# Softmax weights divided by their row sums before the turn, in an attention plus two-MLP kernel

## The chip, the cores and the metric

One core of a Trainium2 chip runs the whole program. The metric is device time in microseconds, from launch to end. The profiled execution also has a span, from its first to its last instruction.

## The reference

```python
def _attn_ref(q, k, v, tau):            # q, k, v: 4 x 8 heads x 576 x 64, fp32
    scale = 1.0 / np.sqrt(q.shape[-1])
    scores = scale * np.matmul(q, k.transpose(0, 1, 3, 2))
    thresh = np.max(scores, axis=-1, keepdims=True) - tau
    scores = np.where(scores >= thresh, scores, -1000000000.0)
    scores = scores - np.max(scores, axis=-1, keepdims=True)
    attn = np.exp(scores)
    attn = attn / (np.sum(attn, axis=-1, keepdims=True) + 1e-09)
    return np.matmul(attn, v)
# reference: x = attention out as 2304 x 512
#   x = elu(x @ moe_w_in) @ moe_w_out        (512 -> 2048 -> 512)
#   out = leaky(x @ moe2_w_in) @ moe2_w_out  (512 -> 2048 -> 512)
```

## The kernel before

The work on attention is cut into 144 *units* (64 queries of two heads at once, so 128 partitions of scores against 576 keys) and 32 *groups* (4 or 5 units of one pair of heads; GROUPS, NE pairs in each). `group` (L417) loads k, q and v of the pair through SyncE's DMA queue (L423, L424, L426) and calls `unit` (L434) for each unit:

- TensorE multiplies q by k into PSUM tile s (L442);
- VectorE scales it into SBUF tile ss and finds the row extreme nm (L446); thr is nm plus tau on GpSimd or VectorE (L449, L451);
- ScalarE applies the threshold with a steep Prelu (L454) and the exponential into tile e, with the row's sum accumulated into a column of su (L457);
- the weights have to be turned so that keys lie on partitions. In the four pairs of the first group index (GP=1) TensorE does it (L472); in the other 28 groups VectorE turns e in blocks of 32 by 32 into t (L464), and 16 DMAs for each group, issued by SyncE, move the 32-partition blocks from t to their place in p (L486).

Then TensorE multiplies p by v into PSUM (L496). The row sums go another way: `row_sums` (L509) takes reciprocals of the group's sums (L511), turns them (L512), stores them in DRAM (L513), and after that has landed reads them back in two DMAs, spread over 64 partitions each (L515), into rb. VectorE multiplies the product by rb into x (L504). Each group so has 22 DMAs on SyncE's queue: 3 loads, 16 for p, 3 for the sums.

The first MLP's products on TensorE (h at L548, y at L591) use three fp32r passes with the hidden half of the weights that is loaded first. Seven blocks of 256 tokens (BESIDE) of them run beside the attention; what is left of the MLPs runs after it. Weights come raw from DRAM (L317) and are split into a high and a low part by GpSimd, ScalarE and VectorE (L321 to L341).

The order is not written by hand: `Order.run` (L110) is a list scheduler that runs when the kernel is built. It holds a cost and a due time (vt, shifted by the constants in KN) for each operation, lets some choose among engines by letters in KN (A ScalarE, D VectorE, P GpSimd), and fixes the order of instructions on every engine. For SyncE it takes ISSUE = 350 ns for each DMA. On the chip each engine, SyncE included, works through its list in order, and an instruction that has to wait holds all behind it. Tiles come from rings: k, q, v, p, t, e and s have two buffers each, ss has three, the product in PSUM one.

Of the kernel before, what the change touches and what calls it, by code (L numbers as in the profile page):

```python
# [10 lines left out]
F32 = mybir.dt.float32  # L11
F32R = mybir.dt.float32r
U32 = mybir.dt.uint32
AF = mybir.ActivationFunctionType
ALU = mybir.AluOpType
# [3 lines left out]
B, H, S, D = 4, 8, 576, 64  # L19
NT, DM, DFF = B * S, H * D, 2048  # L20
NH = B * H
NP = NH // 2
NE = H // 2
HALF = S // 2
# [5 lines left out]
NU = S // 64  # L30
GROUPS = [(b, u0, u1) for b in range(B) for u0, u1 in ((0, 4), (4, NU))]
UM = 5
WT = 32 * UM
BESIDE = 7
GP = 1
SX = 640
LAG = 2
# [5 lines left out]
KN = dict(  # L43
    pad=18, stay=3577.21, late=1.3, margin=0, look=0.00390102, warm=3, tu=2231.35, lead=16053.3, wv0=828.315,
    wv1=194.793, early=4257.91, boff=24778.1, bdt=4649.72, yoff=2581.02, coff=-6478.49, wb=1663.97, w2a=5835.19,
    o1=-2909.85, o2=1357, o3=2931.81, o4=-3826.63, o5=5331.7, o6=-25.7749, mo=-10678.1, ka='PA', kl='PAD', kh='PA',
    ko='D', kt='DP', kx='A', kxl='DP', km='DP', kg='AD', kgl='P', kgl1='D', kd='P', kc='AD')

PE, ACT, DVE, POOL, SP, HOST = "PE", "ACT", "DVE", "POOL", "SP", "HOST"
# [40 lines left out]
class Order:  # L90
# [5 lines left out]
    def op(self, alts, deps=(), uses=(), vt=0.0, lat=0.0):  # L96
        o = Op()
        o.alts = alts if isinstance(alts, list) else [alts]
        o.deps, o.vt, o.lat = [d for d in deps if d is not None], vt, lat
        o.outs, o.done, o.eng, o.seq = [], None, None, len(self.ops)  # L100
        for g in uses:
            if g.back is not None:
                o.deps.append(g.back)
            if not g.users and g.before is not None:
                o.deps.append(g.before.users[0])
            g.users.append(o)
        self.ops.append(o)
        return o

    def run(self):  # L110
        for o in self.ops:
            deps = set()
            for d in o.deps:
                deps.update(d.users if isinstance(d, Gen) else (d,))
            deps.discard(o)
            o.deps, o.left = list(deps), len(deps)
            for d in o.deps:
                d.outs.append(o)
# [17 lines left out]
        while left:  # L136
            best = None
            for e in engines:
                while soon[e] and (soon[e][0][4].done is not None or soon[e][0][0] <= free[e]):
                    t, vt, seq, k, o = heapq.heappop(soon[e])  # L140
# [14 lines left out]
            start, e = best  # L155
            while soon[e] and soon[e][0][0] <= start:
                t, vt, seq, k, o = heapq.heappop(soon[e])
# [8 lines left out]
            vt, seq, k, o = heapq.heappop(now[e])  # L166
# [50 lines left out]
def dve(n):  # L217
    return 69 + 1.042 * n


def dve2(n):
    return 69 + 0.521 * n
# [3 lines left out]
LAND = 2100.0  # L226
ISSUE = 350
HALFP = 105
# [6 lines left out]
def pool_ts(n):  # L235
    return 162 + 0.832 * n
# [12 lines left out]
def moved(packets, size):  # L249
    return packets * (6 + size * 0.0385) / 16 * 1.35  # L250

@with_exitstack
def attn_moe_kernel(ctx, tc, qT, kT, vn, tau, w1i, w1o, w2i, w2o, yp, rsd, out):
    nc = tc.nc
    od = Order()
    op = od.op
# [4 lines left out]
    def ring(pool, n, shape, dtype, tag):  # L261
        return Ring(lambda dt=dtype: (pool[0] if isinstance(pool, list) else pool).tile(shape, dt, tag=tag, name=tag, bufs=n), n)
# [6 lines left out]
    x = const.tile([128, KC, NT], F32, name="x")  # L269
# [18 lines left out]
    PORT = True  # L288

    def sp(packets, size, fn):  # L290
        return (SP, ISSUE, fn, moved(packets, size))

    def pick(who, **alts):
        names = {"A": ACT, "D": DVE, "P": POOL}
        return [(names[c], *alts[c]) for c in who]
# [12 lines left out]
    def copy_of(who, n, dst, src, half=0):  # L308
        return pick(who, A=(actp(n) + 50 * half, lambda: nc.scalar.copy(out=dst(), in_=src())),  # L309
                    D=(dve(n) + HALFP * half, lambda: nc.vector.tensor_copy(dst(), src())))  # L310
# [44 lines left out]
    ya = Ring(lambda: psm.tile([128, 2, 512], F32, tag="y", name="y", bufs=1), 1)  # L355
    s_r = Ring(lambda: psa.tile([128, 2, 512], F32, tag="s", name="s", bufs=2), 2)
    v_ps = Ring(lambda: psa.tile([128, 512], F32, tag="v", name="v", bufs=1), 1)

    ac = sbuf(aes, "ac")
    ap_ = sbuf(aes, "attn")  # L360
    rings = {True: moe_rings(sbuf(aes, "ma"), TA)}
    k_r = ring(ap_, 2, [128, 2, HALF], F32, "k")
    q_r = ring(ap_, 2, [128, 2, 64 * UM], F32, "q")
    v_r = ring(ap_, 2, [128, 2, 5, D], F32, "v")
# [3 lines left out]
    ss_r = Ring(None, 3)  # L368
    es_ = [ac.tile([128, SX], F32, name=f"e{j}") for j in range(2)]
    for t in es_:  # L370
        nc.gpsimd.memset(t[:, S:SX], 0.0)
    e_r = Ring(itertools.cycle(es_).__next__, 2)
    ident = ac.tile([128, 128], F32, name="ident")
    make_identity(nc, ident)
    sm_r = {t: ring(ap_, 4, [128, 1], F32, t) for t in ("nm", "thr")}
    su_r = ring(ap_, 3, [128, UM], F32, "su")
    rc_r = Ring(None, 2)
    st_r = ring(ap_, 2, [128, 32], F32, "st")
    rb_r = ring(ap_, 2, [128, 64 * UM], F32, "rb")

# [5 lines left out]
    ss_r.make = itertools.cycle(sts).__next__  # L386
    sus = [ac.tile([128, 32], F32, name=f"rc{j}") for j in range(2)]
    for t in sus:
        nc.vector.memset(t, 1.0)
    rc_r.make = itertools.cycle(sus).__next__  # L390
    wz = sts[0]
# [22 lines left out]
    xready = {}  # L414
    slot = itertools.count()

    def group(gi, p, vts):  # L417
        b, u0, u1 = GROUPS[gi]
        n, hp = u1 - u0, b * NE + p
        w = 32 * n  # L420
        due = vts[0] - KN["lead"]
        k, q, v = k_r.new(), q_r.new(), v_r.new()
        ld = [op(sp(128, 2304, lambda: nc.sync.dma_start(out=k(), in_=kT[hp])), [], [k], due),  # L423
              op(sp(256, 256 * n, lambda: nc.sync.dma_start(  # L424
                  out=q()[:, :, 0:64 * n], in_=qT[hp][:, :, 64 * u0:64 * u1])), [], [q], due)]
        lv = op(sp(128, 2560, lambda: nc.sync.dma_start(out=v(), in_=vn[hp])), [], [v], due + 8e3)  # L426
        by_pe = gi < GP
        su, pg, tg = su_r.new(), p_r.new(), None if by_pe else t_r.new()
        done, turned = [], []

# [3 lines left out]
        def unit(j, vt):  # L434
            s, ss, e = s_r.new(), ss_r.new(), e_r.new()
            nm, thr = (sm_r[t].new() for t in ("nm", "thr"))

            def qk():
                for h in range(2):
                    for i in range(2):  # L440
                        r = slice(64 * i, 64 * i + 64)
                        nc.tensor.matmul(s()[64 * h:64 * h + 64, i, 0:HALF], q()[r, h, 64 * j:64 * j + 64],  # L442
                                         k()[r, h], start=True, stop=True)
# [13 lines left out]
            o = op((ACT, act(S) + 190, lambda: nc.scalar.activation(  # L457
                out=e()[:, 0:S + 1], in_=ss()[:, 0:S + 1], func=AF.Exp, bias=taun, accum_out=su()[:, j:j + 1])),
                [o], [ss, e, su], vt + KN["o2"])
            done.append(o)  # L460
            cols = slice(32 * j, 32 * j + 32)

            if not by_pe:
# [3 lines left out]
                return  # L467
            t = ya.new()

# [12 lines left out]
        vt = vts[n - 1] + KN["o3"]  # L482
        rb, rgot = row_sums(gi * NE + p, n, su, done, vt + 500)
        got = turned
        if not by_pe:
            got = [op(sp(32, 20 * w, lambda a=a, d=d: nc.sync.dma_start(  # L486
                out=pg()[32 * d:32 * d + 32, 5 * a * w:5 * a * w + 5 * w],
                in_=tg()[32 * a:32 * a + 32, 5 * d * w:5 * d * w + 5 * w])), turned, [pg, tg], vt + KN["o4"])
                for a in range(4) for d in range(4)]
            vt += KN["o5"]  # L490
# [10 lines left out]
        def split(a):  # L501
            return a.rearrange("p (h u i) -> p h u i", h=2, i=32)

        xready[gi, p] = op((DVE, dve(64 * n), lambda: nc.vector.tensor_tensor(  # L504
            out=x[:, p, b * S + 64 * u0:b * S + 64 * u1].rearrange("p (u h i) -> p h u i", h=2, i=32),
            in0=split(ps()[:, 0:64 * n]), in1=split(rb()[:, 0:64 * n]), op=ALU.mult)),
            [o, *rgot], [ps, rb], vt + KN["o6"] + 500)

    def row_sums(at, n, su, done, vt):  # L509
        rb, st, rc = rb_r.new(), st_r.new(), rc_r.new()  # L510
        o = op((DVE, 140, lambda: nc.vector.reciprocal(out=rc()[:, 0:n], in_=su()[:, 0:n])), done, [su, rc], vt)  # L511
        o = op((DVE, 140, lambda: nc.vector.transpose(out=st(), in_=rc())), [o], [rc, st], vt)  # L512
        o = op(sp(128, 128, lambda: nc.sync.dma_start(out=rsd[at].rearrange("a u i -> (a u) i"), in_=st())),  # L513
               [o], [st], vt)
        got = [op(sp(128, 128 * n, lambda h=h: nc.sync.dma_start(  # L515
            out=rb()[64 * h:64 * h + 64, 0:64 * n].rearrange("p (a q) -> p a q", a=2),
            in_=rsd[at, 2 * h:2 * h + 2, 0:n].rearrange("a u i -> a (u i)").partition_broadcast(64))),
            [o], [rb], vt) for h in range(2)]
        return rb, got

# [256 lines left out]
```

## Time and profile before

| | us |
|---|---|
| median of 3 runs | 1160.18 |
| the three runs | 1159.62, 1160.18, 1168.07 |
| profiled execution, its own time | 1164.52 |
| its span | 1162.7 |
| TensorE busy, by the page | 1051.9 |

The profiled execution is 4.3 us above the median of the runs. Engines are called PE (TensorE), PEld (its weight loads), DVE (VectorE), ACT (ScalarE), POOL (GpSimd) and SP (SyncE). SPq rows are DMA issues on SyncE: their length is the time of the issue, not of the transfer. "x16" is a run of 16 merged instructions. An arrow names what the idle time ended on.

### The profile page before, as it was taken

The numbers are of one execution on the slowest core, as the hardware profiler recorded it, in microseconds if no ns is written. First come the engines' busy times: TensorE is split into PE (matmuls) and PEld (weight loads), VectorE is DVE, ScalarE is ACT, GpSimd is POOL, SyncE is SP. The second block draws the span as 40 slices with busy tenths as digits, with TensorE's granted clock in tenths as the row PEclk, the third lists the DMA queues.
The fourth block names the chain that finished last, engine by engine and source line by source line (L and its number), as shares of the span: only waits on it lengthen the run. The fifth ranks groups of instructions, "written<-read, shape, count | busy, mean of one in ns | idle before, by whom it ended". The sixth has DMA issues, their size and how long they took to land.

```text
span 1162.7 us, 17064 instructions
## 1 busy us (share of the span) xinstructions
PE 1051.9 (90%) x6294; PEld 814.4 (70%) x6294; DVE 586.6 (50%) x1201; ACT 508.0 (44%) x1006; POOL 157.5 (14%) x278
## 2 busy tenths in 40 slices
PE   7778777787788778889999999999999999999998
PEld 3455455555566555558888888988888888888898
DVE  6876555655566556628888943686121121121121
ACT  6976555555455555515655532453221221221221
POOL 3454121222111122100111100010000000000000
PEclk9989898989899889989999999999999999999999
DMA  6676666656666666543544411132000000000000
GB/s 217 195 214 178 171 179 178 176 136 179 158 176 158 162 178 176 152 123 109 161 132 161 146 36 37 56 120 79 1 37 1 1 37 1 1 37 1 1 37 20
DMA packets 72435, 125.39 MB, mean 108 GB/s; under 512 B 16032, under 2 KB 37024, under 8 KB 72352
## 3 DMA queue, kind: packets, MB, share of 16 engines
q1 hardware_dynamic: 72352, 124.30, 37.9%
q8 instruction: 50, 0.82, 0.3%
q14 instruction: 33, 0.27, 0.1%
HBM read 72.35 MB, written 9.96 MB: 71 GB/s over the span
## 4 chain that ended last, share of the span: by engine, by line
PE 65%; SPq 15%; DMA 9%; DVE 5%; issue 3%; ACT 2%; POOL 0%; DVEq 0%; ACTq 0%; POOLq 0%
PE y L591 29%; PE h L548 15%; PE hb L548 13%; SPq L486 13%; PE v L496 6%; DMA rb<-rsd_dram 2%; DMA rsd_dram<-st 2%; DMA wraw<-in_w1i_dram 2%; PE s L442 2%; DVE ss L446 2%; DMA p<-t 2%; DVE t L464 1%; ACT e L457 1%; SPq L515 1%; SPq L426 1%
## 5 line engine op out<-in xcount | busy, mean ns | idle before, releaser
L591 PE MATMUL y<-gh,woh 128*128 128x512 f32 (+1 forms) x736 | 255.6, 347 | 2.1 <-ACT ysx L309 1.4
L591 PE MATMUL y<-gl,woh 128*128 128x512 f32 (+1 forms) x736 | 251.4, 342 | 0.0
L591 PE MATMUL y<-gh,wol 128*128 128x512 f32 (+1 forms) x736 | 251.3, 341 | 0.0
L298 DVE TENSOR_TENSOR gl<-g,gh 128x512 fp32r<-128x512 f32 (+1 forms) x128 | 83.3, 651 | 270.6 <-ACT g L574 260.9
L496 PE MATMUL v<-p,v 128*64 128x320 f32 (+1 forms) x640 | 127.9, 496 | 68.8 <-DMA rsd_dram<-st 39.1
L548 PE MATMUL h<-xh,wih 128*128 128x256 f32 (+1 forms) x480 | 164.6, 343 | 14.1 <-DVE g L567 9.4
L591 PEld LDWEIGHTS y<-gh,woh 128*128 128x128 f32 x736 | 138.5, 188 | 34.7 <-issue 14.4
L548 PE MATMUL h<-xl,wih 128*128 128x256 f32 (+1 forms) x480 | 159.0, 331 | 1.3 <-POOL xl L299 1.0
L548 PE MATMUL h<-xh,wil 128*128 128x256 f32 (+1 forms) x480 | 158.3, 330 | 0.0
L454 ACT ACTIVATE ss<-ss,thr 128x576 f32<-128x576 f32 x144 | 110.3, 768 | 105.5 <-DVE thr L451 58.2
L591 PEld LDWEIGHTS y<-gl,woh 128*128 128x128 f32 x736 | 138.6, 188 | 16.2
L591 PEld LDWEIGHTS y<-gh,wol 128*128 128x128 f32 x736 | 138.6, 188 | 16.2
L496 PEld LDWEIGHTS v<-p,v 128*64 128x64 f32 x640 | 62.7, 162 | 122.5 <-issue 64.1
L446 DVE TENSOR_SCALAR_CACHE_REDUCE ss<-s,scl 128x576 f32<-128x576 f32 x144 | 115.1, 800 | 46.6 <-PE s L442 45.3
L464 DVE STREAM_TRANSPOSE t<-e 128x640 f32<-128x640 f32 x128 | 106.7, 839 | 44.7 <-DMA rsd_dram<-st 19.0
L548 PEld LDWEIGHTS h<-xh,wih 128*128 128x128 f32 x480 | 91.6, 191 | 43.4 <-DVE g L567 12.3
L457 ACT ACTIVATE e<-ss,taun 128x577 f32<-128x577 f32 x144 | 111.5, 774 | 13.4 <-DVE t L464 11.1
L442 PE MATMUL s<-k,q 64*64 64x288 f32 x1152 | 97.6, 442 | 12.9 <-DVE ss L446 8.7
L548 PEld LDWEIGHTS h<-xl,wih 128*128 128x128 f32 x480 | 91.8, 191 | 10.2 <-POOL xl L299 1.5
L548 PEld LDWEIGHTS h<-xh,wil 128*128 128x128 f32 x480 | 91.9, 191 | 8.2
L548 PE MATMUL hb<-xl,wih 128*128 128x512 f32 (+1 forms) x256 | 94.5, 369 | 0.0
L548 PE MATMUL hb<-xh,wil 128*128 128x512 f32 (+1 forms) x256 | 94.5, 369 | 0.0
(438 smaller groups left out, 1139.7 us busy)
## 6 DMA issues: line engine op xcount, KB each, us to landing
p<-t SPq DMA_DIRECT2D x256, 100.0 KB, 2.2
p<-t SPq DMA_DIRECT2D x192, 80.0 KB, 2.4
v<-in_vn_dram SPq DMA_DIRECT2D x32, 320.0 KB, 3.7
k<-in_kT_dram SPq DMA_DIRECT2D x32, 288.0 KB, 3.0
wraw<-in_w1i_dram SPq DMA_DIRECT2D x16, 512.0 KB, 4.4
wraw<-in_w1o_dram SPq DMA_DIRECT2D x16, 512.0 KB, 3.6
wraw<-in_w2i_dram SPq DMA_DIRECT2D x16, 512.0 KB, 3.5
wraw<-in_w2o_dram SPq DMA_DIRECT2D x16, 512.0 KB, 3.4
```

What stands on the lines that cost most here:

```text
L298: return pick(who, D=(dve(n), lambda: nc.vector.tensor_tensor(**args()), PORT), P=(pool_tt(n), lambda: nc.gpsimd.tensor_tensor(**args())))
L426: lv = op(sp(128, 2560, lambda: nc.sync.dma_start(out=v(), in_=vn[hp])), [], [v], due + 8e3)
L442: nc.tensor.matmul(s()[64 * h:64 * h + 64, i, 0:HALF], q()[r, h, 64 * j:64 * j + 64], k()[r, h], start=True, stop=True)
L446: o = op((DVE, dve(S) + 160, lambda: nc.vector.tensor_scalar(out=ss()[:, 0:S].rearrange("p (j c) -> p j c", j=2), in0=s()[:, :, 0:HALF], s ...
L454: o = op((ACT, act(S) + 95, lambda: nc.scalar.activation(out=ss()[:, 0:S], in_=ss()[:, 0:S], func=AF.Prelu, bias=thr(), scale=-1.0, alpha= ...
L457: o = op((ACT, act(S) + 190, lambda: nc.scalar.activation(out=e()[:, 0:S + 1], in_=ss()[:, 0:S + 1], func=AF.Exp, bias=taun, accum_out=su( ...
L464: turned.append(op((DVE, dve(SX) + 70, lambda: nc.vector.transpose(out=blocks(tg).rearrange("p d c q -> p c d q")[:, :, :, cols], in_=e(). ...
L486: got = [op(sp(32, 20 * w, lambda a=a, d=d: nc.sync.dma_start(out=pg()[32 * d:32 * d + 32, 5 * a * w:5 * a * w + 5 * w], in_=tg()[32 * a:3 ...
L496: nc.tensor.matmul(ps()[64 * h:64 * h + 64, 0:64 * n], v()[:, h, c, :], blocks(pg)[:, 2 * h:2 * h + 2, c], start=(c == 0), stop=(c == 4))
L515: got = [op(sp(128, 128 * n, lambda h=h: nc.sync.dma_start(out=rb()[64 * h:64 * h + 64, 0:64 * n].rearrange("p (a q) -> p a q", a=2), in_= ...
L548: nc.tensor.matmul(hp(), w_()[:, cs], x_()[:, 0:tb], start=(k == 0 and z == 0), stop=(k == KC - 1 and z == 2))
L591: nc.tensor.matmul(ysl(yg, m), w_()[:, cs], g_()[:, 0:tb], start=(first and z == 0 and share == 0), stop=(last and z == 2 and end))
```

## The change

In each unit a reciprocal of the row's sum is taken on VectorE (128 by 1), and GpSimd multiplies the 576 columns of e by it in place, before e is turned (the scheduler knows a VectorE form too; the constant kn is 'P', so GpSimd has all of them). `row_sums` and its DRAM tensor, its three DMAs a group, its reciprocal and small transpose are gone; the product is copied from PSUM to x by ScalarE (kv='A') where VectorE multiplied. e has three buffers. q is laid out in DRAM by groups, so that a load has 128 packets of 512n bytes where it had 256 of 256n. The 16 block moves are listed by target quarter first. The scheduler's cost of a DMA issue is 400 ns, and 640 ns for block moves, and the constants in KN are others: thr is taken by VectorE alone (kt), the high part of g by ScalarE alone (kg), the high part of x by ScalarE or VectorE (kx), the low bits of the weights by ScalarE or VectorE (kl), and due times differ. The code for moves issued by ScalarE (NA) and for more groups turned by TensorE (PT, AHEAD) is not in use: NA is 0 and PT is empty.

```diff
 KN = dict(
-    pad=18, stay=3577.21, ..., ka='PA', kl='PAD', kh='PA',
-    ko='D', kt='DP', kx='A', kxl='DP', km='DP', kg='AD', kgl='P', kgl1='D', kd='P', kc='AD')
+    pad=18, stay=455.902, ..., ka='PA', kl='AD',
+    kh='PAD', ko='D', kt='D', kx='AD', kxl='DP', km='DP', kg='A', kgl='P', kgl1='D', kd='P', kc='AD', kn='P', kv='A')
...
-ISSUE = 350
+ISSUE = 400
...
-    q_r = ring(ap_, 2, [128, 2, 64 * UM], F32, "q")
+    q_r = ring(ap_, 2, [128, 128 * UM], F32, "q")
...
-    es_ = [ac.tile([128, SX], F32, name=f"e{j}") for j in range(2)]
+    es_ = [ac.tile([128, SX], F32, name=f"e{j}") for j in range(3)]
...
-              op(sp(256, 256 * n, lambda: nc.sync.dma_start(
-                  out=q()[:, :, 0:64 * n], in_=qT[hp][:, :, 64 * u0:64 * u1])), [], [q], due)]
+              op(sp(128, 512 * n, lambda: nc.sync.dma_start(
+                  out=q()[:, 0:128 * n], in_=qT[hp][:, 128 * u0:128 * u1])), [], [q], due)]
...
-                out=e()[:, 0:S + 1], in_=ss()[:, 0:S + 1], func=AF.Exp, bias=taun, accum_out=su()[:, j:j + 1])),
+                out=e()[:, 0:S + 1], in_=ss()[:, 0:S + 1], func=AF.Exp, bias=taun, accum_out=su())),
                 [o], [ss, e, su], vt + KN["o2"])
-            done.append(o)
+            o = op((DVE, 150, lambda: nc.vector.reciprocal(out=su(), in_=su())), [o], [su], vt + KN["o2"])
+            o = op(pick(KN["kn"], P=(pool_ts(S) + 90, lambda: nc.gpsimd.tensor_scalar(
+                            out=e()[:, 0:S], in0=e()[:, 0:S], scalar1=su(), scalar2=1.0, op0=ALU.mult, op1=ALU.mult)),
+                        D=(dve2(S), lambda: nc.vector.tensor_scalar(
+                            out=e()[:, 0:S], in0=e()[:, 0:S], scalar1=su(), scalar2=None, op0=ALU.mult), PORT)),
+                   [o], [su, e], vt + KN["o3"])
...
-        rb, rgot = row_sums(gi * NE + p, n, su, done, vt + 500)
         got = turned
         if not by_pe:
-            got = [op(sp(32, 20 * w, ...)) for a in range(4) for d in range(4)]
+            for z, (a, d) in enumerate((a, d) for d in range(4) for a in range(4)):
...
+                    got.append(op(sp(32, 20 * w, lambda copy=copy: copy(nc.sync), 640), turned, [pg, tg],
+                                  vt + KN["o4"]))
...
-        xready[gi, p] = op((DVE, dve(64 * n), lambda: nc.vector.tensor_tensor(
-            out=x[...], in0=split(ps()[:, 0:64 * n]), in1=split(rb()[:, 0:64 * n]), op=ALU.mult)),
-            [o, *rgot], [ps, rb], vt + KN["o6"] + 500)
-
-    def row_sums(at, n, su, done, vt):
...
+        xready[gi, p] = op(copy_of(KN["kv"], 64 * n, lambda: x[...], lambda: split(ps()[:, 0:64 * n])),
+                           [o], [ps], vt + KN["o6"] + 500)
```

## Rows read from the trace of the kernel before

**Rows 1.** The page: the busy time of each engine, its share of the span, instructions.

```profile
PE 1051.9 (90%) x6294; PEld 814.4 (70%) x6294; DVE 586.6 (50%) x1201; ACT 508.0 (44%) x1006; POOL 157.5 (14%) x278
```

**Rows 2.** Windows: us, busy PE, PEld, DVE, ACT, POOL, PEclk, DMA share, GB/s.

```profile
0.00:65.00 65.00, 47.89 (x386) 24.31 (x386) 49.87 (x134) 51.17 (x106) 28.40 (x44) 0.94 0.66 204
65.00:515.00 450.00, 362.53 (x2824) 250.21 (x2820) 256.05 (x601) 238.45 (x504) 100.81 (x199) 0.92 0.64 167
...
550.00:1162.70 612.70, 608.62 (x2956) 515.53 (x2954) 255.33 (x425) 202.56 (x371) 26.20 (x32) 1.00 0.16 53
```

**Rows 3.** Waits of PE from 65 to 515 us: total, times, longest.

```profile
PE v L496 <- DMA rsd_dram<-st: 39.1, 16, 3.4
PE v L496 <- DMA p<-t: 14.5, 9, 3.7
```

**Rows 4.** Timeline of SP, one turn from 350 to 383 us: start, length.

```profile
350.75 11.55 SPq L486 DMA_DIRECT2D p<-t  x16
362.41 0.53 SPq L513 DMA_DIRECT2D rsd_dram<-st  x1
364.11 1.29 SPq L515 DMA_DIRECT2D rb<-rsd_dram  x2
368.55 0.34 SPq L426 DMA_DIRECT2D v<-in_vn_dram  x1
...
372.93 10.14 SPq L486 DMA_DIRECT2D p<-t  x16
```

**Rows 5.** Timeline of SP: the first and the last run of block moves.

```profile
62.36 5.34 SPq L486 DMA_DIRECT2D p<-t  x8
...
501.65 11.43 SPq L486 DMA_DIRECT2D p<-t  x16
```

**Rows 6.** Issues by line: count, shortest/median/longest ns, first and last start.

```profile
L515 SPq DMA_DIRECT2D rb<-rsd_dram x64: 590/620/1284, 24.4 to 515.6; - x64
L424 SPq DMA_DIRECT2D q<-in_qT_dram x32: 551/620/1221, 1.6 to 459.3; - x32
L423 SPq DMA_DIRECT2D k<-in_kT_dram x32: 327/388/934, 1.2 to 458.9; - x32
```

**Rows 7.** Waits of SP from 65 to 515 us.

```profile
SPq L426 <- PE v L496: 16.1, 10, 3.2
SPq L486 <- DVE t L464: 12.7, 5, 7.5
SPq L515 <- DMA rsd_dram<-st: 9.4, 8, 2.0
```

**Rows 8.** Timeline of PE: two products of 5-unit groups.

```profile
363.97 4.55 PE L496 MATMUL v<-p,v 128*64 128x320 f32 x18 [2.00 <-DMA rsd_dram<-st]
...
476.08 2.88 PE L496 MATMUL v<-p,v 128*64 128x320 f32 x18 [1.66 <-DMA p<-t]
```

**Rows 9.** Groups by form from 65 to 515 us: busy, mean ns, idle before.

```profile
L511 DVE RECIPROCAL rc<-su 128x4 f32<-128x4 f32 x12 | 1.9, 155 | 0.0
L451 DVE TENSOR_SCALAR thr<-nm,taup 128x1 f32<-128x1 f32 x51 | 10.7, 210 | 0.8
L564 POOL TENSOR_SCALAR g<-g 128x256 f32<-128x256 f32 x46 | 18.6, 404 | 96.1 <-ACT g L560 95.8
L299 POOL TENSOR_TENSOR gl<-g,gh 128x256 fp32r<-128x256 f32 x56 | 41.1, 734 | 77.8 <-ACT gh L304 47.4 <-DVE gh L305 20.1 <-issue 4.0
L449 POOL TENSOR_SCALAR thr<-nm,taup 128x1 f32<-128x1 f32 x69 | 18.7, 271 | 149.9 <-DVE ss L446 141.3 <-DVE rc L511 8.2
```

**Rows 10.** GpSimd by line: a usual and the longest one-input pass over 512 columns.

```profile
L302 POOL TENSOR_SCALAR wih<-wb__153 x1: 617/617/617, 10.7 to 10.7; 128x512 fp32r<-128x512 f32 x1
...
L321 POOL TENSOR_SCALAR wa__721<-wraw x1: 1174/1174/1174, 53.7 to 53.7; 128x512 f32<-128x512 f32 x1
```

**Rows 11.** Groups of the whole span: one long two-input VectorE operation, and the usual.

```profile
L298 DVE TENSOR_TENSOR gl<-g,gh 128x512 fp32r<-128x512 f32 (+1 forms) x128 | 83.3, 651 | 270.6 <-ACT g L574 260.9 <-ACT gh L304 8.1 <-PE y L591 0.7
...
L298 DVE TENSOR_TENSOR wol<-wb__6152,woh 128x512 fp32r<-128x512 f32 x1 | 1.7, 1690 | 0.0
```

More of the change, by code (lines that the diff above doesn't have):

```diff
@@ L35 @@
 GP = 1
+AHEAD = 2
+PT = ()
+NA = 0
+ACTI = 150
 SX = 640
@@ L43 @@
 KN = dict(
-    pad=18, stay=3577.21, late=1.3, margin=0, look=0.00390102, warm=3, tu=2231.35, lead=16053.3, wv0=828.315,
-    wv1=194.793, early=4257.91, boff=24778.1, bdt=4649.72, yoff=2581.02, coff=-6478.49, wb=1663.97, w2a=5835.19,
-    o1=-2909.85, o2=1357, o3=2931.81, o4=-3826.63, o5=5331.7, o6=-25.7749, mo=-10678.1, ka='PA', kl='PAD', kh='PA',
-    ko='D', kt='DP', kx='A', kxl='DP', km='DP', kg='AD', kgl='P', kgl1='D', kd='P', kc='AD')
+    pad=18, stay=455.902, late=1.3, margin=0, look=0.00334927, warm=3, tu=2231.35, lead=19463, wv0=558.362,
+    wv1=105.738, early=3916.94, boff=24778.1, bdt=5036.21, yoff=2387.88, coff=7772.05, wb=1110.19, w2a=4797.07,
+    o1=-2440.15, o2=2533.02, o3=4472.77, o4=-3359.29, o5=5750.16, o6=-25.7749, mo=-550.861, ka='PA', kl='AD',
+    kh='PAD', ko='D', kt='D', kx='AD', kxl='DP', km='DP', kg='A', kgl='P', kgl1='D', kd='P', kc='AD', kn='P', kv='A')
 PE, ACT, DVE, POOL, SP, HOST = "PE", "ACT", "DVE", "POOL", "SP", "HOST"
@@ L104, in op @@
             if not g.users and g.before is not None:
-                o.deps.append(g.before.users[0])
+                o.deps.append((g.before,))
             g.users.append(o)
@@ L113, in run @@
             for d in o.deps:
-                deps.update(d.users if isinstance(d, Gen) else (d,))
+                deps.update(d.users if isinstance(d, Gen) else d[0].users[:1] if isinstance(d, tuple) else (d,))
             deps.discard(o)
@@ L252, in attn_moe_kernel @@
 @with_exitstack
-def attn_moe_kernel(ctx, tc, qT, kT, vn, tau, w1i, w1o, w2i, w2o, yp, rsd, out):
+def attn_moe_kernel(ctx, tc, qT, kT, vn, tau, w1i, w1o, w2i, w2o, yp, out):
     nc = tc.nc
@@ L288, in attn_moe_kernel, with sp @@
     PORT = True
-    def sp(packets, size, fn):
-        return (SP, ISSUE, fn, moved(packets, size))
+    def sp(packets, size, fn, issue=ISSUE):
+        return (SP, issue, fn, moved(packets, size))
     def pick(who, **alts):
@@ L368, in attn_moe_kernel @@
     ss_r = Ring(None, 3)
-    es_ = [ac.tile([128, SX], F32, name=f"e{j}") for j in range(2)]
+    es_ = [ac.tile([128, SX], F32, name=f"e{j}") for j in range(3)]
     for t in es_:
         nc.gpsimd.memset(t[:, S:SX], 0.0)
-    e_r = Ring(itertools.cycle(es_).__next__, 2)
+    e_r = Ring(itertools.cycle(es_).__next__, 3)
     ident = ac.tile([128, 128], F32, name="ident")
     make_identity(nc, ident)
[L375 to L379, printed above, removed]
+    sm_r = {t: ring(ap_, 4, [128, 1], F32, t) for t in ("nm", "thr", "su")}
     taut = ac.tile([128, 1], F32, name="taut")
@@ L386, in attn_moe_kernel @@
     ss_r.make = itertools.cycle(sts).__next__
[L387 to L390, printed above, removed]
     wz = sts[0]
@@ L414, in attn_moe_kernel, with s_of @@
     xready = {}
-    slot = itertools.count()
+    slots, unit_no = [], itertools.count()
+    def s_of(i):
+        while len(slots) <= i and len(slots) < NP * NU:
+            slots.append(s_r.new())
+        return slots[i] if i < len(slots) else None
     def group(gi, p, vts):
@@ L423, in group @@
         ld = [op(sp(128, 2304, lambda: nc.sync.dma_start(out=k(), in_=kT[hp])), [], [k], due),
-              op(sp(256, 256 * n, lambda: nc.sync.dma_start(
-                  out=q()[:, :, 0:64 * n], in_=qT[hp][:, :, 64 * u0:64 * u1])), [], [q], due)]
+              op(sp(128, 512 * n, lambda: nc.sync.dma_start(
+                  out=q()[:, 0:128 * n], in_=qT[hp][:, 128 * u0:128 * u1])), [], [q], due)]
         lv = op(sp(128, 2560, lambda: nc.sync.dma_start(out=v(), in_=vn[hp])), [], [v], due + 8e3)
-        by_pe = gi < GP
-        su, pg, tg = su_r.new(), p_r.new(), None if by_pe else t_r.new()
-        done, turned = [], []
+        by_pe = gi < GP or p in PT
+        pg, tg = p_r.new(), None if by_pe else t_r.new()
+        turned = []
         def blocks(g):
@@ L434, in unit @@
         def unit(j, vt):
-            s, ss, e = s_r.new(), ss_r.new(), e_r.new()
-            nm, thr = (sm_r[t].new() for t in ("nm", "thr"))
+            un = next(unit_no)
+            s, ss, e = s_of(un), ss_r.new(), e_r.new()
+            nm, thr, su = (sm_r[t].new() for t in ("nm", "thr", "su"))
             def qk():
@@ L441, in qk @@
                         r = slice(64 * i, 64 * i + 64)
-                        nc.tensor.matmul(s()[64 * h:64 * h + 64, i, 0:HALF], q()[r, h, 64 * j:64 * j + 64],
+                        nc.tensor.matmul(s()[64 * h:64 * h + 64, i, 0:HALF], q()[r, 64 * (n * h + j):64 * (n * h + j) + 64],
                                          k()[r, h], start=True, stop=True)
@@ L467, in unit @@
                 return
-            t = ya.new()
+            s_of(un + AHEAD)
+            t = (ya if gi < GP else s_r).new()
             def tr():
@@ L482, in group, with copy @@
         vt = vts[n - 1] + KN["o3"]
-        rb, rgot = row_sums(gi * NE + p, n, su, done, vt + 500)
         got = turned
         if not by_pe:
[L486 to L489, printed above, removed]
+            got = []
+            for z, (a, d) in enumerate((a, d) for d in range(4) for a in range(4)):
+                to = pg, slice(32 * d, 32 * d + 32), slice(5 * a * w, 5 * a * w + 5 * w)
+                fr = tg, slice(32 * a, 32 * a + 32), slice(5 * d * w, 5 * d * w + 5 * w)
+                def copy(q, to=to, fr=fr):
+                    q.dma_start(out=to[0]()[to[1], to[2]], in_=fr[0]()[fr[1], fr[2]])
+                if z * NA // 16 != (z + 1) * NA // 16:
+                    got.append(op((ACT, ACTI, lambda copy=copy: copy(nc.scalar)), turned, [pg, tg], vt + KN["o4"],
+                                  lat=2500))
+                else:
+                    got.append(op(sp(32, 20 * w, lambda copy=copy: copy(nc.sync), 640), turned, [pg, tg],
+                                  vt + KN["o4"]))
             vt += KN["o5"]
@@ L502, in split @@
             return a.rearrange("p (h u i) -> p h u i", h=2, i=32)
-        xready[gi, p] = op((DVE, dve(64 * n), lambda: nc.vector.tensor_tensor(
-            out=x[:, p, b * S + 64 * u0:b * S + 64 * u1].rearrange("p (u h i) -> p h u i", h=2, i=32),
-            in0=split(ps()[:, 0:64 * n]), in1=split(rb()[:, 0:64 * n]), op=ALU.mult)),
-            [o, *rgot], [ps, rb], vt + KN["o6"] + 500)
-    def row_sums(at, n, su, done, vt):
[L510 to L519, printed above, removed]
+        xready[gi, p] = op(copy_of(KN["kv"], 64 * n, lambda: x[:, p, b * S + 64 * u0:b * S + 64 * u1].rearrange(
+            "p (u h i) -> p h u i", h=2, i=32), lambda: split(ps()[:, 0:64 * n])), [o], [ps], vt + KN["o6"] + 500)
     def conv_x(t0, tb, deps, vt, reg):
@@ L749 @@
     qt = q.transpose(0, 1, 3, 2).reshape(NP, 2, D, S).transpose(0, 2, 1, 3)
-    lay["qT"] = _np.concatenate([qt, qt], 1)
+    qt = [qt[..., 64 * a:64 * b].reshape(NP, D, -1) for _, a, b in GROUPS[:2]]
+    lay["qT"] = _np.concatenate([_np.concatenate(qt, -1)] * 2, 1)
     kt = k.transpose(0, 1, 3, 2).reshape(NP, 2, D, 2, HALF).transpose(0, 3, 2, 1, 4)
@@ L770 @@
     yp = nc.dram_tensor("yp_dram", (128, KC, NT), F32, kind="Internal").ap()
-    rsd = nc.dram_tensor("rsd_dram", (len(GROUPS) * NE, 4, 32, 32), F32, kind="Internal").ap()
     o = nc.dram_tensor("out_0_dram", (DM, NT), F32, kind="ExternalOutput").ap()
     with _tile.TileContext(nc) as tc:
-        attn_moe_kernel(tc, *args, yp, rsd, o)
+        attn_moe_kernel(tc, *args, yp, o)
     r = _run(nc, [arrays], core_ids=[0])
```

## The prediction

> **What bounds the kernel now.** I read the page's busy line first, then the windows, then the waits of TensorE, then SyncE's own timeline. The busy line says TensorE 90% [rows 1], but the windows split this in two [rows 2]. From 550 us to the end TensorE is busy 608.6 of 612.7 us at a granted clock of 1.00: the MLPs alone, which the change does not touch. From 65 to 515 us, the attention, it is busy 362.5 of 450 us at 0.92. So what can be won lies there: 87 us idle, and the clock. With two levels of clock (2.4 and 1.2 GHz) a mean of 0.92 is 16% of the stretch at the lower one, 72 us, in which work of 36 us at full clock takes twice as long.
>
> The waits name the product v as the one that stands: 39.1 us on the store of the sums and 14.5 on the block moves [rows 3]. The first name misleads. The product at L496 needs p and v and not the sums; the store is simply the next DMA behind the 16 block moves on the same queue, and the two land together. In the timeline the moves' issues end at 362.3, the store is issued at 362.41, and the product starts at 363.97 [rows 4, 8]. The true releaser is the last block move.
>
> Why is it late? SyncE's timeline shows one issue after another. I added up its rows from 62.4 us to 514.9 us, 452.5 us; the runs of block moves at both ends are shown [rows 5]. The 448 block moves take 298.5 us (0.67 each), 28 stores of sums 15.0, 56 reads of sums 37.1, 25 q loads 15.5, 25 k loads 11.1, 26 v loads 11.5, stores of y and weights 7.9: 396.5 us of 452.5. The 56 us between them are 46 us of waits over 0.2 us and 10 us of small gaps. So SyncE's queue sets the pace, at 16.1 us a group, and TensorE, with 362, comes next. Some turns are a ring, too: in the one shown the product frees the buffer for the v load at 368.55, and the scores that TensorE had behind the product feed the turn for which SyncE waits until 372.93.
>
> **The change part by part.** All sums are against the profiled execution, 1164.5 us, which is 4.3 us over the median.
>
> *Transfers of sums removed.* On SyncE 15.0 + 37.1 = 52.1 us of issue go (a store 0.53 us, two reads 1.29 [rows 4]), with some 5 us of the small gaps beside them. The wait of the reads for the store to land goes as well, 9.4 us [rows 7]. All of it is on the queue that sets the pace: -66.
>
> *q by groups.* The load becomes like the k load, 128 packets: 0.388 in place of 0.620 us (medians [rows 6]), 25 x 0.23 = -6. The bounds are no gain, if the length does not follow the packets, and -7 at the shortest k row.
>
> *The reciprocals.* 128 more of them in this stretch on VectorE; a 128x4 one takes 155 ns, a 128x1 tensor operation 210 [rows 9]: 20 to 27 us. What goes are 27 old reciprocals, 27 small transposes and 27 multiplications by rb; at 0.16, 0.21 and some 0.36 us each (the last estimated as a bit over half of the 651 ns of a two-input operation over 512 columns [rows 11]) that is 20 us. The thr of GpSimd move over, 69 x 0.21 = 14.5 us. VectorE goes from 256 to about 274 us of a stretch of some 390: room enough, so nothing on the path. If that cover is gone it costs these 18 us.
>
> *GpSimd's multiplication.* A one-input pass takes 404 ns for 256 columns and 617 for 512 [rows 9, 10], so about 0.67 us for 576; the longest row, 1174, is the upper end. 128 x 0.67 = 86 us; GpSimd loses 18.7 us of thr and some weight passes, and goes from 101 to about 168 us, under half of the stretch. It is off the bound by work, but it lengthens each unit's chain by reciprocal, multiplication and two handovers, 1.0 to 1.6 us. That shows where SyncE already waits for the turn, five times [rows 7]: +6. Elsewhere the third e buffer and the two t buffers hide it. If GpSimd is still in a gl subtraction (0.734 us) it is 0.7 more each time; bounds 0 to +20 us in all.
>
> *Copy by ScalarE.* 28 copies of 320 columns or fewer go to an engine busy 238 of 450 us, and wait for the product only, not for rb. Nothing, between -5 (a block's first h starts earlier) and +5 (ScalarE held behind the product).
>
> *The planner.* It took 350 ns for an issue that lasts 670, so it put v on TensorE's list when p was not yet there. With 640 it puts other products ahead. This gives no more room on SyncE, but shortens the stalls of TensorE, and a product without a long stall ahead runs faster: 4.55 us after a stall, 2.88 elsewhere, for the same shape [rows 8]. The other order of block moves (target quarter first) and the other due times I price at zero, between -10 and +10 us, as no row shows them. The start (65 us, bound by weights) and the tail stay, within 5 us either way.
>
> *The sum.* SyncE's stretch becomes 452.5 - 66 - 6 + 6 = 386 us. TensorE has 362 at the present clock, 326 at the full one, so it is over 84% full; two lists this full that wait for one another lose a little, and I add 5 us, as the waits for v buffers (16.1 us [rows 7]) suggest. 391, so -62 us: 1164.5 - 62 = 1102.5 for the profiled execution, and 1098 us by the median.
>
> A sentence that stands apart: the Trainium skill, in "DMA: Bandwidth & Descriptors", section "Issuing engines are not separate DMA queues", says that issuing on several engines saves only sequencer time, "which is usually small relative to the DMA itself". By that rule the 52 us of issue would be worth little. The trace does not agree here: 0.67 us of issue, 448 times, fill two thirds of the stretch.
>
> **The rivals.**
>
> A. *TensorE becomes the bound.* If the new order removes all stalls, the stretch falls to TensorE's 362 us at the present clock, or, with fewer stalls, to what SyncE needs without any wait: 396.5 - 52 - 6 + some 6 of gaps = 345. Take 357: -95, 1065 us by the median. For it: a planner with true issue costs. Against it: both lists would have to be almost gapless.
>
> B. *The ring is the bound.* In the turn shown, moves, landing, product, v load, scores, exponentials and turn follow each other, 22.2 us from run to run [rows 4], and most sums' issues lie beside that ring. Then about 1.2 us (the store's wait and issue) for half of the groups and 2 us for the others are won, and 1.3 us of chain given back in half: 28 x 0.95 = 27 us, 1133. Against it: all waits over 0.2 us on SyncE make only 46 us in 28 turns, so most turns are not such rings.
>
> C. *The transfers are hidden anyway.* If it is latency alone that counts, only the 9.4 us of waits go: 1151. The rule quoted above would have it so. The full queue speaks against it.
>
> D. *VectorE is held behind GpSimd.* VectorE's list is in order: a turn that waits for the multiplication holds the next units' scaling. Its work would be 274 us plus the hold, 128 times. From a hold of 176/128 = 1.38 us a unit it passes the 450 us of before. The chain allows that: multiplication 0.67 to 1.17, two handovers, half the time a gl of 0.73 ahead, so 1.0 to 2.2. At 1.7, 274 + 218 = 492, +42 us: 1202. A row that shows such a hold: a two-input operation of VectorE of 1690 ns where 651 is the mean [rows 11]. The Trainium skill, "SBUF — State Buffer", section "SBUF: two separate sides", has GpSimd and some VectorE operations lock a shared port pair for a whole instruction; the long row agrees, though the turn and the scaling, with one input, showed no such rows. Against D: with three e buffers the turn can stand one unit later in the list, where e is ready.
>
> **How the numbers follow.** The forecast, SyncE still the pace, has 0.54; A 0.19, B 0.15, C 0.06, D 0.06. The range has to hold 8 of 10: down to 1062, which takes in A as priced and leaves out only gapless lists below it, and up to 1140, past B at 1133 and past the forecast with all upper bounds (+14 chain, +6 q, +5, +10, so 1133). C, D and a part of A are left out, near 0.18. A measurement of this kernel can tell about 1% (12 us) from no change. Faster by more: the forecast, A and B, 0.88. Within 1%: C, 0.06. Slower: D, 0.06.
>
> **What would show it.** Right: no stores or reads of sums on SyncE; block moves still 0.6 to 0.7 us each and back to back; the last of them issued near 453 us; TensorE from 65 us on over 88% busy with a granted clock above 0.92; GpSimd's multiplication near 0.67 us. A is right if v waits under 15 us in all; B, if SyncE's waits grow past 80 us; C, if the stretch is still 440 us. D shows as VectorE waiting on GpSimd before the turn for over 100 us, with scores waiting for the scaling. Wrong above all would be block moves whose issue takes another time in the new order, or a changed tail after 550 us.

## The result and the profile after

The changed kernel takes 1079.05 us (median of four runs, 1074.30 to 1082.72) against 1162.08 in the runs of before that go with it: 0.928 of the time, with a 95% interval of 0.922 to 0.933. The profiled execution took 1082.72 us.

The page's busy line, the windows (columns as in [rows 2]), and the longest of TensorE's waits for the product (as in [rows 3], from 60 to 437 us), each of the kernel after:

```profile
PE 1028.9 (95%) x6294; PEld 802.5 (74%) x6294; DVE 605.8 (56%) x1374; ACT 501.4 (46%) x1017; POOL 225.8 (21%) x317
```

```profile
0.00:60.00 60.00, 44.68 (x367) 23.17 (x367) 45.79 (x133) 49.68 (x103) 35.39 (x48) 0.97 0.60 190
60.00:430.00 370.00, 340.07 (x2802) 235.99 (x2803) 259.80 (x713) 252.21 (x549) 179.05 (x257) 0.97 0.73 193
...
470.00:1080.70 610.70, 607.09 (x2948) 514.03 (x2947) 269.19 (x473) 184.69 (x340) 9.96 (x11) 1.00 0.17 52
```

```profile
PE v L514 <- DMA p<-t: 7.2, 8, 2.4
```

The attention has shrunk from some 450 to 370 us; the tail is what it was. In the stretch TensorE's idle time fell from 87 to 30 us, and its granted clock rose from 0.92 to 0.97. The product's long waits for block moves are almost gone.

SyncE's timeline after, about one group and a half (compare [rows 4]), and the row of all block moves by line, with first and last start:

```profile
262.83 5.59 SPq L500 DMA_DIRECT2D p<-t  x9
268.46 0.58 SPq L425 DMA_DIRECT2D k<-in_kT_dram  x1
269.08 0.44 SPq L426 DMA_DIRECT2D q<-in_qT_dram  x1
269.62 4.33 SPq L500 DMA_DIRECT2D p<-t  x7
274.04 0.53 SPq L428 DMA_DIRECT2D v<-in_vn_dram  x1
274.61 6.21 SPq L500 DMA_DIRECT2D p<-t  x9
280.86 0.58 SPq L425 DMA_DIRECT2D k<-in_kT_dram  x1
```

```profile
L500 SPq DMA_DIRECT2D p<-t x448: 507/589/2061, 67.4 to 434.2; - x150
```

Each issue starts within 0.1 us of the end of the one before: the queue is full. The group shown passes in 12.4 us (its k load stands at 268.46, the next at 280.86); the mean of the 28 is 13.1, where it was 16.1. I added the rows up from the first block move to the end of the last. As in the forecast, a run of merged moves counts as one row, with the gaps inside it (44 ns between most moves, now and then a wait); a move's issue by itself takes 0.618 us in the mean before and 0.627 after.

| us | before | after |
|---|---|---|
| start of the first block move | 62.4 | 67.4 |
| first to end of last block move | 450.7 | 367.3 |
| block moves, 448 | 297.9 | 303.4 |
| the same, mean of one | 0.665 | 0.677 |
| store and reads of sums | 50.3 | none |
| k, q and v loads | 38.1 | 41.1 |
| stores of y, loads of weights | 5.8 | 5.3 |
| waits over 0.2 us | 45.1 | 7.8 |
| gaps below that | 13.6 | 9.7 |
| end of the last move to the end of the span | 649.7 | 645.9 |

So 83.4 us come from SyncE's stretch, 3.8 from the tail, and 5.1 are lost at the start. Two things went from the stretch: issues, and waits. The experiments take them apart.

### The profile page after: what moved, and what is told of

The parts are those of the page before. It is cut to its first block, busy times and chain, and to the rows that moved or that the text cites. A ratio compares the mean times of both kernels' runs of the same rounds, so it can differ in the third digit from the quotient of the medians.

```text
span 1080.7 us, 17082 instructions
## 1 busy us (share of the span) xinstructions
PE 1028.9 (95%) x6294; PEld 802.5 (74%) x6294; DVE 605.8 (56%) x1374; ACT 501.4 (46%) x1017; POOL 225.8 (21%) x317
## 4 chain that ended last, share of the span: by engine, by line
PE 81%; SPq 6%; DMA 5%; DVE 4%; ACT 2%; issue 2%; POOL 0%; DVEq 0%; ACTq 0%
PE y L595 34%; PE h L552 20%; PE hb L552 14%; PE v L514 6%; SPq L500 6%; PE s L445 5%; DMA q<-in_qT_dram 2%; DMA p<-t 1%; DMA v<-in_vn_dram 1%; DVE ss L449 1%; ACT e L460 1%; DMA wraw<-in_w1o_dram 1%; ACT ss L457 1%; DVE g L571 1%; PE v L394 0%
## 5 line engine op out<-in xcount | busy, mean ns | idle before, releaser
L552 PE MATMUL h<-xh,wih 128*128 128x256 f32 (+1 forms) x480 | 168.0, 350 | 14.6 <-DVE g L571 9.8
L595 PEld LDWEIGHTS y<-gl,woh 128*128 128x128 f32 x736 | 138.9, 189 | 16.1
L552 PEld LDWEIGHTS h<-xh,wih 128*128 128x128 f32 x480 | 91.0, 190 | 57.3 <-issue 16.1
L460 ACT ACTIVATE e<-ss,taun 128x577 f32<-128x577 f32 x144 | 111.3, 773 | 32.2 <-DVE t L472 27.7
L464 POOL TENSOR_SCALAR e<-e,su 128x576 f32<-128x576 f32 x144 | 108.0, 756 | 80.6 <-DVE su L463 73.4
L472 DVE STREAM_TRANSPOSE t<-e 128x640 f32<-128x640 f32 x128 | 103.8, 831 | 32.2 <-DMA p<-t 21.7
L514 PE MATMUL v<-p,v 128*64 128x320 f32 (+1 forms) x640 | 95.5, 422 | 12.8 <-DMA p<-t 7.2
L552 PE MATMUL hb<-xh,wih 128*128 128x512 f32 (+1 forms) x256 | 94.5, 369 | 0.0
```

Of the source, the lines that this page charges most:

```text
L460: o = op((ACT, act(S) + 190, lambda: nc.scalar.activation(out=e()[:, 0:S + 1], in_=ss()[:, 0:S + 1], func=AF.Exp, bias=taun, accum_out=su())),
L464: o = op(pick(KN["kn"], P=(pool_ts(S) + 90, lambda: nc.gpsimd.tensor_scalar(out=e()[:, 0:S], in0=e()[:, 0:S], scalar1=su(), scalar2=1.0, o ...
L472: turned.append(op((DVE, dve(SX) + 70, lambda: nc.vector.transpose(out=blocks(tg).rearrange("p d c q -> p c d q")[:, :, :, cols], in_=e(). ...
L514: nc.tensor.matmul(ps()[64 * h:64 * h + 64, 0:64 * n], v()[:, h, c, :], blocks(pg)[:, 2 * h:2 * h + 2, c], start=(c == 0), stop=(c == 4))
L552: nc.tensor.matmul(hp(), w_()[:, cs], x_()[:, 0:tb], start=(k == 0 and z == 0), stop=(k == KC - 1 and z == 2))
L595: nc.tensor.matmul(ysl(yg, m), w_()[:, cs], g_()[:, 0:tb], start=(first and z == 0 and share == 0), stop=(last and z == 2 and end))
```

## The experiments

*Queue theory*: SyncE's list sets the pace, before and after; what is taken from it is worth about its length. *Plan theory*: the new plan makes the gain, and the transfers hardly count. *Rival A*: after the change TensorE is the bound.

**1. The true issue costs alone**, in the kernel before:

```diff
-ISSUE = 350
+ISSUE = 400
...
-                in_=tg()[...])), turned, [pg, tg], vt + KN["o4"])
+                in_=tg()[...]), 640), turned, [pg, tg], vt + KN["o4"])
```

> The kernel before with one thing changed: its scheduler takes 400 ns for a DMA issue and 640 ns for a block move, as after; due times, sums' transfers and all work as before. Queue theory (SyncE's 396 us of issues set the pace, and only its 46 us of waits can be won by a plan): faster by 0 to 30 us, 1130 to 1162. Plan theory (the false cost was what made the product late, the transfers hardly mattered): most of the 83 us, under 1110. If a plan made for other due times is only disturbed: within 15 us of 1162 on either side.

1128.87 us, 0.971 of before (0.969 to 0.973). The sums' transfers are all there, and the block moves, by line, run

```profile
L486 SPq DMA_DIRECT2D p<-t x448: 507/589/1880, 63.5 to 476.4; - x150
```

a stretch of 413.5 us. Its issues are what they were; its waits over 0.2 us add up to 5.3 us, where before had 45.1. The gain, 32 us, is just above the 0 to 30 us that the queue theory gave: a plan can win SyncE's waits, and won nearly all. It is far from the 83 of the plan theory.

**2. The whole plan of after, in the kernel before**: the issue costs above and all constants in KN.

> The kernel before with the issue costs and all the constants in KN of after (due times and engine letters), with the sums' transfers and the multiplication by rb kept. Queue theory: SyncE's issues remain 396 us, so at best its 46 us of waits go and some lead at the start: 1115 to 1150. Plan theory: 1080 to 1100.

1137.70 us, 0.978 (0.974 to 0.982): within the queue theory's range, and 9 us slower than the costs alone. The stretch is 423.2 us. In this kernel the other constants of after do harm.

**3. The kernel after with the old plan**: ISSUE 350 for all DMAs, KN of before, with kn='P' and kv='A' added.

> The kernel after with the issue cost of 350 ns for all DMAs and the constants in KN of before (kn and kv added). Queue theory: the 52 us of issue and the waits for the store are gone whatever the plan, so 62 us of gain stay, less what the old plan leaves as waits: 1090 to 1115. Plan theory: 1130 to 1160.

1135.72 us, 0.978 (0.975 to 0.981), slower than either number I gave for the queue theory and within the plan theory's range. The list has no sums' transfers any more, yet the stretch is 409.9 us. SyncE's waits from 65 to 480 us say where the removed 52 us went:

```profile
SPq L428 <- PE v L514: 47.4, 17, 5.0
SPq L500 <- DVE t L472: 10.4, 4, 3.6
```

The waits over 0.2 us add up to 62.3 us. SyncE stands before v loads for TensorE's product to free the buffer. Before had 16.1 us of these [rows 7]. My reading of this, which no run shows by itself: with the false cost, the scheduler expects block moves to be out early and lines up work in an order that SyncE then meets too early or too late.

**4. True costs, old constants**: the kernel after with KN of before, but 400 and 640 ns.

> The kernel after with the constants in KN of before (kn and kv added), but with the true issue costs kept (400 and 640 ns). If the issue cost is what took SyncE's waits away, its waits fall from the 62 us of the run with the false cost to about 10, and the time to 1080 to 1095. If the due times did it, the waits stay over 40 us and the time over 1120.

1082.09 us, 0.930 (0.926 to 0.934): the same as after, with a stretch of 369.3 us and waits of 14.4. So in the kernel after only the cost of an issue counts of the plan; the due times and engine letters make no difference that shows. The two effects now stand in a square, stretch in us:

| | false issue cost | true issue cost |
|---|---|---|
| sums through DRAM | 450.7 (before) | 413.5 (1) |
| division ahead of the turn | 409.9 (3) | 369.3 (4), 367.3 (after) |

Each is worth about 37 to 46 us, in either order. The lower row has the whole rest of the change and not only the missing transfers; experiments 5, 6, 8 and 9 test its parts. The layout of q and the copy by ScalarE were not run by themselves.

**5. The three DMAs put back into the kernel after**, with nothing that uses them:

```diff
+        o = op(sp(128, 128, lambda: nc.sync.dma_start(out=rsd[at]..., in_=sth)), turned[-1:], [], vt + 500)
+        for h in range(2):
+            op(sp(128, 128 * n, lambda h=h: nc.sync.dma_start(out=rb()[64 * h:64 * h + 64, ...], in_=rsd[at, ...]...)),
+               [o], [rb], vt + 500)
```

> The kernel after with three DMAs a group put back on SyncE, a store of 128 by 32 constants to DRAM and two reads spread over 64 partitions each; nothing uses what they bring, the scheduler knows of them, and all the rest is as after. Queue theory: SyncE's list is longer by 52 us of issue and 28 waits of the reads for the store, so 50 to 65 us slower than after, 1130 to 1145. Rival A (TensorE is the bound after the change): its 340 us in 370 leave only some of that visible, under 25 us, below 1105.

1129.59 us, 0.971 of before (0.969 to 0.974) where after has 0.928: 50 us slower, at the low end of what the queue theory gave, and more than rival A allows. The moves, by line:

```profile
L512 SPq DMA_DIRECT2D p<-t x448: 507/589/1566, 69.0 to 480.0; - x150
```

The stretch is 411.5 us. No engine uses what these transfers bring; the reads' waits for the store make 4.7 us, and the issues of the three DMAs 53.4. So this is issue time on a full queue, and hardly any latency. The Trainium skill, "DMA: Bandwidth & Descriptors", section "Issuing engines are not separate DMA queues", calls the sequencer's time for a DMA usually small relative to the DMA itself. The trace agrees for one move (an issue of 0.59 us, 2.3 to 3.2 us to landing, medians); but transfers overlap and issues do not, and here the issue is what costs.

**6. Without the division**: no reciprocal and no multiplication (the computation lacks the division by the row sums).

> The kernel after without the reciprocals and without GpSimd's multiplication: the weights stay undivided, so the division is left out of the computation. Queue theory: the multiplication lies beside SyncE's list, within 8 us of 1079. Rival D in a weaker form (VectorE held behind GpSimd costs part of the stretch): 15 us faster or more.

1081.28 us, 0.929 (0.926 to 0.933), the same as after. GpSimd's 144 multiplications and VectorE's 144 reciprocals cost nothing that can be measured. After's row for the multiplications, by line, and the wait that rival D needed:

```profile
L464 POOL TENSOR_SCALAR e<-e,su x144: 736/746/1242, 12.0 to 418.6; 128x576 f32<-128x576 f32 x144
```

```profile
L472 DVE STREAM_TRANSPOSE t<-e 128x640 f32<-128x640 f32 x126 | 102.1, 831 | 32.2 <-DMA p<-t 21.7 <-POOL e L464 4.9 <-DMA k<-in_kT_dram 2.9
```

The last is a group by form from 60 to 437 us: the turn waited 4.9 us in all for GpSimd.

**7. The multiplication on VectorE**: kn='D'.

> The kernel after with the multiplication on VectorE in place of GpSimd (kn='D'). VectorE gets 128 operations of 0.37 us or more on top of 260 in 370 us, GpSimd loses 93. Queue theory: SyncE's list is the same, so within 10 us of 1079 as long as VectorE stays below 330. If VectorE's list, with waits, is the next bound: 1090 to 1110.

1102.05 us, 0.947 (0.944 to 0.950). Neither reading was right about the place. The moves and the multiplication, by line, and one multiplication in the timeline with GpSimd's work beside it:

```profile
L500 SPq DMA_DIRECT2D p<-t x448: 507/589/2455, 88.6 to 454.4; - x150
```

```profile
L466 DVE TENSOR_SCALAR e<-e,su x144: 501/517/1433, 14.1 to 441.1; 128x576 f32<-128x576 f32 x144
```

```profile
73.61 1.27 POOL L303 TENSOR_TENSOR wil<-wb__786,wih 128x512 fp32r<-128x512 f32 x1 [0.21 <-ACT wih L308]
...
73.76 1.43 DVE L466 TENSOR_SCALAR e<-e,su 128x576 f32<-128x576 f32 x1
```

The stretch is 366.4 us, as after: SyncE still sets the pace there. But it begins at 88.6 instead of 67.4. All 21 us are lost in the start, where VectorE also has the weights' passes: up to the first block move it is busy 70.7 us of 88.6, where after has 52.1 of 67.4. TensorE's granted clock there is 0.79 against 0.92, and how much of the loss is the clock's stays open.

One multiplication took up to 1433 ns where 517 is the median, and the trace shows why. The 82 with no GpSimd operation beside them took 501 to 522 ns. In 32 cases a GpSimd operation was under way and went on for over 0.2 us; each of these multiplications ended 0.31 to 0.32 us after that operation's end, whatever its start (in the rows above, at 75.19 and 74.88). The Trainium skill, "SBUF — State Buffer", section "SBUF: two separate sides", has some VectorE operations and GpSimd's exclude each other on a shared port pair, for a whole instruction. The trace agrees: the multiplication got its turn when GpSimd's operation was over.

**8. Two buffers for e** in the kernel after, in place of three.

> The kernel after with two buffers for e in place of three. If the third buffer hides the longer chain (exponential, reciprocal, multiplication, turn), SyncE waits for turns and it is 10 to 40 us slower, 1090 to 1120, with waits of ScalarE's exponential for the turn well above the 28 us of after. If not: within 8 us of 1079.

1090.81 us, 0.938 (0.937 to 0.940), 12 us slower, at the edge of the range given, but not for the reason given:

```profile
L500 SPq DMA_DIRECT2D p<-t x448: 507/589/1910, 77.8 to 442.2; - x150
```

The stretch is 365.0 us, as after, with 8.4 us of waits; the start is 10 us longer. The exponential's waits for the turn went from 27.7 to 34.1 us only. The third buffer earns its place before the first block move, and nothing measurable after it.

**9. Source quarter first**, the moves in the order of before.

> The kernel after with the block moves in the order of before (source quarter first). The order was priced at zero within 10 us: 1070 to 1089 and an issue of 0.66 to 0.69 us either way. If the order matters, the mean issue differs by 0.03 us or more, 13 us over 448 moves.

1077.05 us, 0.926 (0.924 to 0.928), mean row 0.677 us a move, as after: the order makes no difference that shows.

**10 to 12. Fewer issues on SyncE**: some of the 16 moves issued by ScalarE, first 4 with the 150 ns that the code has for such an issue, then 4 and 2 with 640.

```diff
-NA = 0
-ACTI = 150
+NA = 4
+ACTI = 640
```

> The kernel after with 4 of the 16 block moves of a group issued by ScalarE. Queue theory: SyncE's 352 us of issues fall by 112 x 0.68 = 76 us, and TensorE, 340 us busy in the 370 of its stretch, sets the end: 15 to 30 us faster than after, 1050 to 1065. Rival A (TensorE is already the bound): within 8 us of 1079. If an issue takes ScalarE 0.6 us as it does SyncE, it gets 67 us on top of 252: still below TensorE; if it holds ScalarE's list until the turn is done, the exponentials come late and it is slower than 1085.

> As the run with 4 of 16 block moves issued by ScalarE, but with 640 ns as the scheduler's cost of such an issue in place of 150. If that run was slow because the scheduler again had a false issue cost (its ScalarE issues took about 0.6 us each), this one is 15 us or more faster than its 1107, and by the queue theory faster than after: 1055 to 1075. If ScalarE's list has no room for 67 us of issues whatever the plan, or the two queues make each other's issues longer (SyncE's went from 0.68 to 0.76 us there): 1085 to 1110.

> The kernel after with 2 of the 16 block moves of a group issued by ScalarE, at a cost of 640 ns in the scheduler. SyncE's list loses 38 us, ScalarE's gets 34. Queue theory: 352 - 38 = 314 us of issues pass below TensorE's 340, so 10 to 20 us faster than after, 1060 to 1070. If the longer issues eat it: 1075 to 1090.

1106.74 (0.952, 0.949 to 0.955), 1103.25 (0.949, 0.947 to 0.952) and 1101.48 us (0.948, 0.945 to 0.951): all over 20 us slower than after, and the true cost hardly helped. In the last one the moves on SyncE and ScalarE are, by line,

```profile
L500 SPq DMA_DIRECT2D p<-t x392: 507/589/1731, 67.4 to 448.6; - x196
...
L500 ACTq DMA_DIRECT2D p<-t x56: 514/580/913, 68.2 to 441.3; - x56
```

and SyncE's longest wait from 60 to 437 us

```profile
SPq L500 <- DMA p<-t: 30.6, 17, 3.2
```

SyncE's list got shorter, but the gaps over 0.2 us between its issues, those inside merged rows too, add up to 76 us with two moves and to 112 and 115 with four, where after has 13. The issues themselves did not become longer: one takes 0.609 us in the mean with two and 0.615 and 0.602 with four, against 0.627. The 0.76 in the expectation above was the length of merged rows, with waits inside.

ScalarE's moves were not late, either: in all 28 groups of each run they were issued over 5 us ahead of SyncE's last one. What SyncE waits for is their landing. In this program the DMAs of both engines share eight completion semaphores, and before each of its DMAs SyncE waits until the one before on the same semaphore has landed. With two moves on ScalarE, 21 of SyncE's gaps, 38.7 us, end just as a move of ScalarE lands on the semaphore of SyncE's next DMA; with four they make 48 us (150 ns) and 32 (640). The scheduler takes no such wait into account. I expected a gain from this and got a loss, of which these waits are the largest part that I can name; the rest stays open. These runs do not tell how near TensorE's own limit lies below 367 us.

## Why the prediction held, and which steps were off

**What bounds.** The reading of before was right: the last block move released the product, not the store named in [rows 3], and SyncE's list set the pace. Experiment 5 shows the length of the list at work with no data hanging on it, and in experiments 1, 2, 4 to 9 the stretch is the issues plus 13 to 27 us of waits and gaps, whatever the other engines do. My sum of before's rows was a little off: some stood in two views and were counted twice. It is 393 us of issues, not 396.5, and 60 between them.

**Sums removed, -66.** Mis-sized: 44 us of stretch from experiment 5 to after, 46 from experiment 1. The issues of the sums and some 4 us of gaps went as worked out, but the issues that stay became longer: block moves by 0.012 us with the gaps in their runs (5.4 in all), k loads from 0.445 to 0.573 in the mean (3.1), v loads from 0.441 to 0.542 (2.6). That gives back 11 us. For the k loads the rows show on what it hangs: behind a block move one takes 0.58 us (median, in the kernel after and in experiment 5), behind a store of sums 0.39 in the kernel before and 0.44 in experiment 5. With the stores gone, the k loads stand behind block moves. And the 9.4 us of waits were not this term's to give: with the old plan the waits grew.

**q, -6.** Mis-sized. The q load's median fell, from 0.620 to 0.441 us, but its mean only to 0.553, as some rows take up to 1.46; that is 2 us in the stretch. With the longer k and v loads the three together cost 3 us more.

**The planner, 0.** The step that failed, though the time came out within the range. I wrote that the true costs give "no more room on SyncE" and only shorten stalls of TensorE. They took SyncE's waits from 45 to 5 us, alone and at once: 37 us of stretch in experiment 1, 41 between 3 and 4. Most of these waits were SyncE's for a v buffer or a turn [rows 7], that is, for the lists of TensorE and VectorE, which the scheduler had laid out by a false time of the moves. I had read some of them as a ring in the hardware's work [rows 4, 7], when they went with another order. The forecast kept 36 us of waits, added 6 for the chain and 5 for two full lists; of these some 48 us 8 were there.

The forecast's stretch of 391 us was 338 of issues, 5 of gaps and 48 of waits; measured are 350, 10 and 8. So two errors of opposite sign met: 40 us of waits too many, and 16 us of issues and gaps too few. With the first alone the forecast would have been 1058, below the range that I gave; that it came within 19 us of the time is in part luck.

**GpSimd and the chain, +6.** Nothing (experiment 6). GpSimd was busy just under half of the time (179 of 370 us), as said, though one multiplication took 0.75 us where 0.67 was estimated from the 256- and 512-column rows.

**TensorE's clock.** The products did get faster: the mean of one of their matmuls fell from 496 to 422 ns, as the page has it:

```profile
L514 PE MATMUL v<-p,v 128*64 128x320 f32 (+1 forms) x640 | 95.5, 422 | 12.8 <-DMA p<-t 7.2
```

But the two products of [rows 8] did not show what I read from them, as both stood behind a stall, of 2.00 and of 1.66 us. What differs is the granted clock, 0.63 in the slow one and 1.00 in the other (windows of before, columns as in [rows 2]):

```profile
363.97:368.52 4.55, 4.55 (x22) 2.02 (x25) 0.09 (x1) 0.00 (x0) 0.00 (x0) 0.63 0.19 36
476.08:478.96 2.88, 2.88 (x22) 1.58 (x25) 0.84 (x1) 0.10 (x2) 0.00 (x0) 1.00 0.21 69
```

**Start and tail.** At the edge of the 5 us given (5.1 lost, 3.8 won). That the start is a stage of its own, bound by VectorE and the e buffers, I had not priced; experiments 7 and 8 lose all their time there.

**Rivals.** A's own sign came true, 12.8 us of waits before v by the page, and TensorE is 92% busy; but the sign was badly chosen, since a full SyncE queue with a good order gives it as well. Experiment 5 rules A out as the pace. B fell with experiment 1: the ring dissolves by reordering. C fell with 5. D fell with 6 and the 4.9 us. Its long row [rows 11] was read rightly: a GpSimd subtraction (L299) ran beside it, as in experiment 7. But VectorE's turn and its scaling took no longer beside GpSimd's work than without (medians 840 and 833 ns, 808 and 809).

## What to carry to other kernels

Where many small DMAs are issued by one engine, add up its issue rows over the stretch and set the sum beside the stretch: a nearly full list is the bound even if every transfer is short and hidden, and a wait named after one DMA may belong to its neighbour on the queue. If a build-time scheduler orders the work, compare its costs with the rows first: one wrong constant was worth as much here as three DMAs a group. A mean taken from merged rows holds the waits inside them, so look at single issues before calling an issue slow. And waits of the bounding engine are not part of its work; ask what a correct order would leave of them before keeping them in a sum.

## What was not expected of the hardware

A block move's issue took ScalarE as long as SyncE (medians 580 and 589 ns), and SyncE's issues kept their length while ScalarE issued too. With both engines issuing, one waited for the other's transfers, by the shared semaphores (38.7 us in the run with two moves). An issue's length went with the one before it: a k load took 0.58 us behind a block move and 0.39 behind a store. A VectorE multiplication of 0.51 us took up to 1.43 beside a GpSimd operation, and ended 0.31 us after it. The moves of 100 KB took longer to land than before (medians 2.2 and 3.2 us, by the page) and those of 80 KB did not (2.4 and 2.3); why, no run here shows.
